# Attention and two feed-forward layers on one core: chunk 3's second-layer pass behind the first layer's passes, with seven products in both of its matmuls, and joint softmax statistics of two heads

## The chip, the core and the metric

The kernel runs on one core of one Trainium2 chip. The metric is device time in microseconds (us) of one execution. Engines are named as in the profile: PE (TensorE) multiplies matrices, PEld is its weight load, DVE (VectorE) and ACT (ScalarE) work element by element, POOL is GpSimd, SP issues the DMAs. PE accumulates in PSUM, which has eight banks of 512 float32 columns; all else lies in SBUF or DRAM.

## What is computed

The attention is causal by blocks of 64 positions, for 4 batches of 8 heads with 576 positions of 64 numbers each:

```python
scores = scale * np.matmul(q, k.transpose(0, 1, 3, 2))
mask = block_i >= block_j
scores = np.where(mask, scores, -1000000000.0)
scores = scores - np.max(scores, axis=-1, keepdims=True)
attn = np.exp(scores)
attn = attn / (np.sum(attn, axis=-1, keepdims=True) + 1e-09)
return np.matmul(attn, v)
```

Its output, 2304 tokens of 512 numbers, goes through two layers of width 2048. The first has `h = x @ w_in`, `g = h * tanh(softplus(h))`, `g @ w_out`; the second has `h = max(x @ w_in, 0)`, `h * h @ w_out`. All inputs and outputs are float32.

## The kernel before

**Numbers.** A float32 matrix is held as two float16 parts, a high and a low one, and a product takes three matmuls: high by high, low by high, high by low.

**Chunks and passes.** The tokens are cut into six chunks of 384 (`CH1`). A pass `(l, c)` takes chunk c through layer l. It has eight groups j; in each, the first matmul makes 256 of the 2048 inner columns, ACT applies the layer's function, and the second matmul adds their share to the output. `PASSES` is the order of the twelve passes, (0, 0), (0, 1), (0, 2), (1, 0), (1, 1), (0, 3), (1, 2), (1, 3), (0, 4), (0, 5), (1, 4), (1, 5), and the second matmul of a group runs one group behind the first one.

**Two ways for each matmul.** The plain way is line 1352 in the first matmul (`first_half`) and line 1464 in the second (`second_half`): 24 matmuls of 384 columns in each group. The other way replaces a 2x2 block product by seven products of blocks, with sums of blocks formed beforehand: `first_seven` (line 1385), for the passes in `SEVEN`, has 42 matmuls of 192 columns in a group; `second_seven` (line 1503), for the passes in `BOTH`, has 36 of 192 columns and 12 pieces, six of 128 and six of 64, because one of its seven products is spread over the spare columns of three accumulators. It needs seven blocks of the activation, of which DVE forms four by subtraction (line 1445) before it splits all seven, 1344 columns, into high and low part (lines 1121 to 1123 and 818); the plain way splits 768 columns. It accumulates in six banks, of which two, `bank`, otherwise serve the attention.

**Weights.** The float16 parts are kept in DRAM (`wspill`) and read for each group (`weights`, line 1246): 512 KB, or 384 KB where only three of four blocks are wanted. Block sums are formed by `upgrade` (lines 1206 to 1215), stored in `uspill` and read for each group (`sums_of`, line 1225). `UP` says in which pass which sums are formed. From pass number `KEEP` on, the sums for the second layer's first matmul stay in SBUF once read.

**Attention.** `attention_hi` (line 865) handles two heads and 384 queries in three tiles of 128. PE writes the scores of head 0 into one bank and of head 1 into the other (line 909); each head's maximum is taken by its own DVE reduction (`peak`, line 922), multiplied by the scale (`low`, line 927); ACT takes the exponential and sums it (`expo`, line 933); DVE adds a small constant (line 943), takes the reciprocal (line 945), and the result is split and transposed by DMA (`finish`, lines 953 to 958). The third tile's diagonal block is computed with the first tile, copied out of PSUM for each head (`tail`, line 791), and its maximum and sum are merged later (`merge`, line 940).

**Order.** Each step is recorded as a task with its dependencies, and a packed table, `PLAN`, holds the sequence of all tasks and the engine of each that has a choice. Each engine runs its own instructions in that order. So a step that waits holds up what is queued behind it on its engine.

## Time and profile before

| | us |
|---|---|
| median of 3 runs | 860.58 (860.36 to 862.75) |
| the profiled execution's own time | 862.35 |
| its span | 860.6 |
| PE busy | 845.9 |
| DVE busy | 757.8 |
| ACT busy | 620.8 |
| POOL busy | 62.8 |

The span runs from the first to the last instruction that was profiled; what lies around it is the difference to the execution's own time, 1.75 us. Busy time is the time in which an engine had at least one instruction in work. Matmuls overlap, so a single one's duration is longer than the time by which it delays the next one; that time is read from the starts of groups that follow each other.

### The profile page before, as it was taken

To read this page: it belongs to the slowest core of one execution; us is meant where nothing else is said; L and a number is where in the kernel's file an instruction comes from. 1 tells how busy PE (TensorE), PEld (TensorE's weight loads), DVE (VectorE), ACT (ScalarE), POOL (GpSimd) and SP (SyncE) were. 2 spreads that over 40 slices of the span, in tenths; PEclk is the share of its full clock that TensorE was granted. 3 is DMA by queue.
4 is the path that set the end of the run, shared out by engine and by line. 5 is a ranking of instruction groups with operands and counts; after the bars stand their busy time and mean duration, and the time that the engine had idled before them with its cause. 6 is when DMAs were issued, how large, how long until landed. Compare 5 with 4: busy or idle time off the path is not lost.

```text
span 860.6 us, 19000 instructions
## 1 busy us (share of the span) xinstructions
PE 845.9 (98%) x7233; PEld 606.5 (70%) x7233; DVE 757.8 (88%) x1831; ACT 620.8 (72%) x1231; POOL 62.8 (7%) x68
## 2 busy tenths in 40 slices
...
GB/s 348 385 349 196 222 242 246 288 303 309 262 280 170 284 251 205 235 287 257 277 293 335 264 230 281 231 262 195 256 242 279 180 243 190 264 229 253 190 204 79
DMA packets 163930, 217.23 MB, mean 252 GB/s; under 512 B 107520, under 2 KB 125952, under 8 KB 163840
## 3 DMA queue, kind: packets, MB, share of 16 engines
...
q14 instruction: 34, 0.28, 0.1%
...
## 4 chain that ended last, share of the span: by engine, by line
PE 76%; DVE 6%; ACT 4%; DMA 3%; issue 1%; ACTq 0%; DVEq 0%
PE acc L1464 30%; PE hp L1385 22%; PE hp L1352 11%; PE acc L1503 5%; PE bank L1018 3%; PE bank L909 3%; PE bank L1503 2%; ACT pad L933 1%; DMA qk<-in_qp_dram 1%; DMA arena<-wspill 1%; DMA wspill<-arena 1%; DVE arena L818 1%; DVE pb L818 1%; ACT L1357 1%; DMA late<-pb 1%
## 5 line engine op out<-in xcount | busy, mean ns | idle before, releaser
L1464 PE MATMUL acc<-g,arena 128*128 128x384 f16 x1560 | 300.4, 326 | 2.1 <-DVE late L1478 0.8
L1464 PEld LDWEIGHTS <-arena 128*128 128x128 f16 x1560 | 146.7, 98 | 87.2 <-issue 7.0
L1385 PEld LDWEIGHTS <-arena 128*128 128x128 f16 x1194 | 101.2, 98 | 15.3 <-DMA arena<-wspill 1.8
L1352 PE MATMUL hp<-xt,first 128*128 128x384 f16 x528 | 101.2, 326 | 0.4 <-ACT h L1357 0.3
L818 DVE SCALAR_TENSOR_TENSOR g<-h,cst,g 128x768 f16<-128x768 f32 x72 | 73.3, 1018 | 4.9 <-ACT g L1121 3.7
L1352 PEld LDWEIGHTS <-first 128*128 128x128 f16 x528 | 49.1, 97 | 40.4 <-issue 9.2
L1385 PEld LDWEIGHTS <-first 128*128 128x128 f16 x816 | 69.5, 98 | 7.2 <-issue 0.4
L1352 PE MATMUL hp<-xt,arena 128*128 128x384 f16 x384 | 73.8, 326 | 0.0
L818 DVE SCALAR_TENSOR_TENSOR pb<-pad,st,pb 128x384 f16<-128x384 f32 (+2 forms) x96 | 71.8, 751 | 1.2 <-ACT pb L953 1.1
L933 ACT ACTIVATE pad<-bank,st,sq 128x448 f32<-128x448 f32 (+1 forms) x96 | 64.9, 680 | 4.4 <-DVE st L927 3.6
L1385 PE MATMUL hp<-arena 128*128 128x192 f16 x660 | 65.8, 246 | 0.0
L1406 ACT ACTIVATE h<-h,cst 128x576 f32<-128x576 f32 x40 | 30.9, 774 | 43.0 <-DVE h L1404 39.9
L953 ACT ACTIVATE pb<-pad,st 128x640 f16<-128x640 f32 (+2 forms) x72 | 51.1, 718 | 7.5 <-DVE st L945 5.3
L1385 PE MATMUL hp<-xt,arena 128*128 128x192 f16 x534 | 54.8, 246 | 1.6 <-DMA arena<-wspill 1.6
L1357 ACT ACTIVATE h<-hp,cst 128x384 f32<-128x384 f32 x76 | 41.6, 575 | 17.2 <-PE hp L1352 14.3
L922 DVE TENSOR_REDUCE st<-bank 128x1 f32<-128x448 f32 (+1 forms) x96 | 52.5, 571 | 0.9 <-PE bank L913 0.4
L1352 PEld LDWEIGHTS <-arena 128*128 128x128 f16 x384 | 36.1, 98 | 24.2 <-issue 0.8
L1385 PE MATMUL hp<-arena,first 128*128 128x192 f16 x480 | 50.0, 246 | 0.0
L1121 ACT ACTIVATE g<-h,cst 128x768 f16<-128x768 f32 x38 | 35.4, 931 | 10.2 <-PE acc L1464 8.5
L1402 ACT ACTIVATE h<-hp,cst 128x192 f32<-128x192 f32 x40 | 16.7, 416 | 34.9 <-PE hp L1385 29.9
L1210 DVE TENSOR_TENSOR arena<-arena 128x256 f32<-128x256 f32 x96 | 41.2, 430 | 0.6
L1503 PEld LDWEIGHTS <-arena 128*128 128x128 f16 x504 | 37.5, 98 | 0.0
...
## 6 DMA issues: line engine op xcount, KB each, us to landing
...
```

The lines of the kernel that those rows point to most:

```text
L818: return sch.add("DVE", c_dve(n) + 62 * ap, lambda: nc.vector.scalar_tensor_tensor(dst(), a(), s() if ap else s, c(), op0, op1), r=r, w=w, ...
L922: t = sch.add("DVE", c_dve(o1 - o0), lambda hd=hd: nc.vector.reduce_max(st.t[:, 2 * j + hd:2 * j + hd + 1], pp.t[hd][:, o0:o1], axis=AX.X) ...
L933: t = sch.add("ACT", c_act(o1 - o0, True, 3), lambda hd=hd: nc.scalar.activation(pf[hd].t[r0:, k0:k0 + o1 - o0], view(hd)[r0:, o0:o1], AF. ...
L953: "ACT": ("ACT", c_act(n, False, 1), lambda pb=pb, pv=pv, s=s: nc.scalar.activation(pb.t[:, 0:i + 1, 0, :], pv(), AF.Copy, scale=s()), False),
L1121: "ACT": ("ACT", c_act(n, False, 1), lambda: nc.scalar.activation(dst(0), src(), AF.Copy, scale=s()), False),
L1210: plus(ENG["ts"], 256, lambda e, o=o, x=x, y=y, op=op: e.tensor_tensor(b(o), b(x), b(y), op), [], [q])
L1352: nc.tensor.matmul(out=hp.t[:, 0:n], lhsT=w.t[:, f % 2, a, 128 * k:128 * k + 128], rhs=x.t[:, c, k, 0:n], start=k == 0 and i == 0, stop=k ...
L1357: sch.add("ACT", c_act(n, True, 1), lambda f=f, o=o, hp=hp: nc.scalar.activation(h.t[:, o * n:o * n + n], hp.t[:, 0:n], (AF.Mish, AF.Relu) ...
L1385: nc.tensor.matmul(out=bank.t[:, o:o + z], lhsT=lhs, rhs=x.t[:, c, ks[k], :], start=start and k == 0 and i == 0, stop=k == 1 and i == 2, s ...
L1406: sch.add("ACT", c_act(3 * z, False, 1), lambda: nc.scalar.activation(h.t[:, z:2 * n], h.t[:, z:2 * n], fn, scale=hs()), r=[(cst, (HS, j)) ...
L1464: nc.tensor.matmul(out=acc.t[:, 0:n], lhsT=wo.t[:, f % 2, a, 128 * m:128 * m + 128], rhs=g.t[:, c, f % 2 * n:f % 2 * n + n], start=f == 0 ...
L1503: nc.tensor.matmul(out=acc[bank].t[:, o:o + c1 - c0], lhsT=lhs, rhs=g.t[:, c, z * b + c0:z * b + c1], start=j == 0 and (bank, o) in first ...
```

## The change

Chunk 3's second-layer pass (1, 3) moves from behind (1, 2) to behind (0, 5), so that the second layer's last three passes stand together, and it joins `BOTH`. `KEEP` and `UP` follow: the sums that stay are read in (1, 3), and the block sums for the second matmul are formed in the same two passes, (0, 4) and (0, 5), which are one place earlier now. The two banks become one tile of 1024 columns, and one reduction takes the maxima of both heads. One column block `st` holds the statistics of all three tiles of a pair of heads: the constant and the reciprocal of the first two tiles are taken for four columns at once, and both their splits come behind that; the third tile's two maxima are merged by one operation with the scaling; its small sum takes the constant on POOL (line 988 of the changed kernel), and DVE adds the large one. The diagonal block is copied out for both heads by one instruction. `PLAN` is a new table throughout.

```diff
@@ -46,13 +46,13 @@
-Y_AT = ["a", "p", "s", "p", "p", "s"]
-X_AT = {(0, 0): "c", (0, 1): "b", (0, 2): "c", (1, 0): "b", (1, 1): "c", (0, 3): "y", (1, 2): "z", (1, 3): "y", (0, 4): "z", (0, 5): "y", (1, 4): "z", (1, 5): "y"}
+Y_AT = ["a", "p", "s", "p", "t", "s"]
+X_AT = {(0, 0): "c", (0, 1): "b", (0, 2): "c", (1, 0): "b", (1, 1): "c", (0, 3): "y", (1, 2): "z", (0, 4): "y", (0, 5): "z", (1, 3): "y", (1, 4): "z", (1, 5): "y"}
-KEEP = 10
+KEEP = 9
 SEVEN = {(0, 3), (1, 2), (1, 3), (0, 4), (0, 5), (1, 4), (1, 5)}
-BOTH = {(1, 4), (1, 5)}
-UP = {4: [(0, 0, j) for j in range(8)], 5: [(1, 0, j) for j in range(8)], 8: [(1, 1, j) for j in range(4)], 9: [(1, 1, j) for j in range(4, 8)]}
+BOTH = {(1, 3), (1, 4), (1, 5)}
+UP = {4: [(0, 0, j) for j in range(8)], 5: [(1, 0, j) for j in range(8)], 7: [(1, 1, j) for j in range(4)], 8: [(1, 1, j) for j in range(4, 8)]}
...
@@ -675,7 +673,7 @@
-    R["xm"] = sb("xm", [128, 8], F32, 5)
+    R["xm"] = sb("xm", [128, 8], F32, 6)
...
@@ -747,7 +745,9 @@
-    bank = [psp.tile([128, 512], F32, tag=f"bank{i}", name=f"bank{i}") for i in range(2)]
+    banks = psp.tile([128, 1024], F32, tag="bank", name="bank")
+    bank = [banks[:, 512 * i:512 * i + 512] for i in range(2)]
+    pairs = banks.rearrange("p (h c) -> p h c", h=2)
...
@@ -915,76 +915,81 @@
-        both = lambda st, j, r0=0: st.t[r0:, 2 * j:2 * j + 2]
-
-        def peak(st, j, pp, o0, o1):
-            for hd in range(2):
-                t = sch.add("DVE", c_dve(o1 - o0), lambda hd=hd: nc.vector.reduce_max(st.t[:, 2 * j + hd:2 * j + hd + 1], pp.t[hd][:, o0:o1], axis=AX.X),
-                            w=[(pp, hd), (st, (j, hd))])
-                t.banks = (hd,)
-
-        def low(st, r):
-            sch.add("DVE", 69.0, lambda: nc.vector.tensor_scalar(both(st, 2), both(st, 0), sq.t[:, 5:6], None, ALU.mult),
-                    r=[(sq, 5), *r], w=[(st, 2)], lat=70.0)
-
-        def expo(st, j, pp, r0, o0, o1, pf, k0):
-            view = lambda hd: pp.t[hd] if j == 4 else pp.t[:, hd]
+        st = R["st"].new()
+        two = lambda j, n=2: st.t[:, 2 * j:2 * j + n]
+        TOP, SUM = (0, 2, 3), (4, 5, 7)
+
+        def peak(j, pp, o0, o1):
+            sch.add("DVE", 70.0 + c_dve(2 * (o1 - o0)), lambda: nc.vector.reduce_max(two(j), pairs[:, :, o0:o1], axis=AX.X),
+                    w=[(pp, 0), (pp, 1), (st, (j, 0)), (st, (j, 1))]).banks = (0, 1)
+
+        def low(j, n):
+            keys = [(st, (k, hd)) for k in range(j, j + n) for hd in range(2)]
+            sch.add("DVE", 69.0, lambda: nc.vector.tensor_scalar(two(j, 2 * n), two(j, 2 * n), sq.t[:, 5:6], None, ALU.mult),
+                    r=[(sq, 5)], w=keys, lat=70.0)
+
+        def expo(j, b, pp, o0, o1, pf, k0):
+            view = lambda hd: pp.t[:, hd] if j == 6 else pp.t[hd]
             for hd in range(2):
                 t = sch.add("ACT", c_act(o1 - o0, True, 3), lambda hd=hd: nc.scalar.activation(
-                    pf[hd].t[r0:, k0:k0 + o1 - o0], view(hd)[r0:, o0:o1], AF.Exp, bias=st.t[r0:, 4 + hd:5 + hd], scale=sq.t[r0:, 4:5],
-                    accum_out=st.t[r0:, 2 * j + hd:2 * j + hd + 1]), r=[(st, 2), (sq, 4)], w=[(pp, hd), (st, (j, hd)), (pf[hd], k0)], table="exp")
-                t.banks = (hd,) if j == 4 else ()
-
-        def merge(st, j, op, r, w):
-
-            sch.add("DVE", 69.0, lambda: nc.vector.tensor_tensor(both(st, j), both(st, j), both(st, j + 1), op), r=r, w=w)
-
-        def finish(i, st, pf):
-            sch.add("DVE", 69.0, lambda: nc.vector.tensor_scalar(both(st, 6), both(st, 4), 1e-9, 1.0 / PSC, ALU.add, ALU.mult),
-                    r=[(st, (4, 0)), (st, (4, 1))], w=[(st, 6)])
-            sch.add("DVE", 75.0, lambda: nc.vector.reciprocal(both(st, 7), both(st, 6)), r=[(st, 6)], w=[(st, 7)], lat=70.0)
+                    pf[hd].t[:, k0:k0 + o1 - o0], view(hd)[:, o0:o1], AF.Exp, bias=st.t[:, 2 * b + hd:2 * b + hd + 1], scale=sq.t[:, 4:5],
+                    accum_out=st.t[:, 2 * j + hd:2 * j + hd + 1]), r=[(st, (b, hd)), (sq, 4)], w=[(pp, hd), (st, (j, hd)), (pf[hd], k0)], table="exp")
+                t.banks = () if j == 6 else (hd,)
+
+        def finish(i, pf):
+            k = SUM[i - 2]
...
-                s = lambda hd=hd: st.t[:, 14 + hd:15 + hd]
+                s = lambda hd=hd: st.t[:, 2 * k + hd:2 * k + hd + 1]
...
-                    [(st, 7), f], [(pb, 0)])
+                    [(st, (k, hd)), f], [(pb, 0)])
-                    ALU.mult, ALU.subtract, [(st, 7), f, (pb, 0)], [(pb, 1)], 1)
+                    ALU.mult, ALU.subtract, [(st, (k, hd)), f, (pb, 0)], [(pb, 1)], 1)
...
         scale_of(R["qm"].new())
+        pfs = {}
         for i in (2, 3):
             n = tile_keys(i)
-            pp, st, pf = R["ab"].new(), R["st"].new(), [R["pf", i].new() for _ in range(2)]
+            pp, pfs[i] = R["ab"].new(), [R["pf", i].new() for _ in range(2)]
             scores(pp, (i, 0, 0, n, True), *([(4, n, 448, 576, True)] if i == 2 else []))
             if i == 2:
-                last, tail = R["st"].new(), R["tl"].new()
+                tail = R["tl"].new()
                 steps.append(halves(vs, v3, sv, R["vm"].new()))
-            peak(st, 0, pp, 0, n)
+            peak(TOP[i - 2], pp, 0, n)
             if i == 2:
-                for hd in range(2):
-                    t = copy(ENG["tail"], 128, lambda hd=hd: tail.t[:, hd], lambda pp=pp, n=n, hd=hd: pp.t[hd][:, n:n + 128], [], [(pp, hd), (tail, hd)], True)
-                    t.banks = (hd,)
-                sch.add("DVE", c_dve(256), lambda: nc.vector.reduce_max(both(last, 1), tail.t, axis=AX.X), r=[(tail, 0), (tail, 1)], w=[(last, 1)])
-            low(st, [(st, (0, 0)), (st, (0, 1))])
-            expo(st, 4, pp, 0, 0, n, pf, 0)
-            finish(i, st, pf)
+                copy(ENG["tail"], 256, lambda: tail.t, lambda n=n: pairs[:, :, n:n + 128], [], [(pp, 0), (pp, 1), (tail, 0), (tail, 1)], True).banks = (0, 1)
+                low(0, 1)
+                expo(SUM[0], 0, pp, 0, n, pfs[i], 0)
+                sch.add("DVE", c_dve(256), lambda: nc.vector.reduce_max(two(1), tail.t, axis=AX.X),
+                        r=[(tail, 0), (tail, 1)], w=[(st, (1, 0)), (st, (1, 1))])
+            else:
+                low(1, 2)
+                expo(SUM[1], 2, pp, 0, n, pfs[i], 0)
+        keys = [(st, (k, hd)) for k in (4, 5) for hd in range(2)]
+        sch.add("DVE", 70.0, lambda: nc.vector.tensor_scalar(two(4, 4), two(4, 4), 1e-9, 1.0 / PSC, ALU.add, ALU.mult), w=keys)
+        sch.add("DVE", 79.0, lambda: nc.vector.reciprocal(two(4, 4), two(4, 4)), w=keys, lat=70.0)
+        for i in (2, 3):
+            finish(i, pfs[i])
         pp, pf = R["ab"].new(), [R["pf", 4].new() for _ in range(2)]
         scores(pp, (4, 0, 0, 448, False))
-        peak(last, 0, pp, 0, 448)
-        merge(last, 0, ALU.max, [(last, 1), (last, (0, 0)), (last, (0, 1))], [(last, 0)])
-        low(last, [(last, 0)])
-        expo(last, 5, tail, 0, 0, 128, pf, 448)
-        expo(last, 4, pp, 0, 0, 448, pf, 0)
-        merge(last, 4, ALU.add, [(last, (5, 0)), (last, (5, 1))], [(last, (4, 0)), (last, (4, 1))])
-        finish(4, last, pf)
+        peak(3, pp, 0, 448)
+        keys = [[(st, (k, hd)) for hd in range(2)] for k in (1, 3, 6, 7)]
+        sch.add("DVE", 69.0, lambda: nc.vector.scalar_tensor_tensor(two(3), two(3), sq.t[:, 5:6], two(1), ALU.mult, ALU.min),
+                r=[(sq, 5), *keys[0]], w=keys[1], lat=70.0)
+        expo(6, 3, tail, 0, 128, pf, 448)
+        sch.add("POOL", 492.0, lambda: nc.gpsimd.tensor_scalar(two(6), two(6), 1e-9, 1.0 / PSC, ALU.add, ALU.mult), w=keys[2])
+        expo(7, 3, pp, 0, 448, pf, 0)
+        sch.add("DVE", 69.0, lambda: nc.vector.scalar_tensor_tensor(two(7), two(7), 1.0 / PSC, two(6), ALU.mult, ALU.add), r=keys[2], w=keys[3])
+        sch.add("DVE", 75.0, lambda: nc.vector.reciprocal(two(7), two(7)), w=keys[3], lat=70.0)
+        finish(4, pf)
...
@@ -1809,10 +1814,10 @@
-PASSES=[(0, 0), (0, 1), (0, 2), (1, 0), (1, 1), (0, 3), (1, 2), (1, 3), (0, 4), (0, 5), (1, 4), (1, 5)]
+PASSES=[(0, 0), (0, 1), (0, 2), (1, 0), (1, 1), (0, 3), (1, 2), (0, 4), (0, 5), (1, 3), (1, 4), (1, 5)]
...
@@ -1820,7 +1825,7 @@
-ATT = [[2, 1, 0, 0.0, 0.093], [3, 2, 1, 1.938, 4.83], [4, 5, 7, 0.035, 1.615], [5, 6, 8, 0.044, 1.181]]
+ATT = [[2, 1, 0, 0.0, 0.093], [3, 2, 1, 1.938, 4.83], [4, 4, 7, 0.035, 1.615], [5, 5, 8, 0.044, 1.181]]

```

Line numbers of the changed kernel are five higher than before from `second` on. Three places show what the new table does to the order.

DVE inside the pass (1, 3). Before, `g` is the activation of the group, split whole; `h` is that of the next one:

```order
L1397 TENSOR_TENSOR h_7240<-first,hp_123 128x192
L1398 TENSOR_TENSOR h_7240<-h_7240,hp_123 128x192
L1286 TENSOR_TENSOR xs<-xs 128x2x192 x3
L1404 TENSOR_TENSOR h_7240<-first,hp_123 128x384
L1286 TENSOR_TENSOR xs<-xs 128x2x192
L1123 TENSOR_SCALAR g_7302<-h_7240,cst_6196 128x768
L818 SCALAR_TENSOR_TENSOR g_7302<-h_7240,cst_6196,g_7302 128x768
```

Now, with the activation in `pad` and its split in `pt`:

```order
L1403 TENSOR_TENSOR pad<-pad,hp_123 128x192
L1450 TENSOR_TENSOR pad<-pad 128x192
L1121 TENSOR_SCALAR cst_7136<-cst_7136 128x1
L1450 TENSOR_TENSOR pad<-pad 128x192
L1344 TENSOR_SCALAR cst_7136<-wst_1503,cst_7136 128x16
L830 TENSOR_REDUCE xm_8201<-xs 128x1
L1409 TENSOR_TENSOR pad<-first,hp_123 128x384
L818 SCALAR_TENSOR_TENSOR pt<-pad,cst_7136,pt 128x1344
L1450 TENSOR_TENSOR pad<-pad 128x192 x2
```

The split has 1344 columns in place of 768, and subtractions of 192 columns (L1450) stand between.

POOL while the attention of a middle chunk runs. Before, only splits of activations (`g`) and of queries and keys (`q`) and a square stand there:

```order
L1122 TENSOR_SCALAR arena<-late,cst_6196 128x384
L1122 TENSOR_SCALAR g_6346<-h_6259,cst_4183 128x768
L1122 TENSOR_SCALAR g_6495<-h_6382,cst_4183 128x768
L895 TENSOR_SCALAR q_15_6545<-qk,sq_6503 128x384
L1368 TENSOR_TENSOR h_7042<-h_7042 128x768
```

Now the small sums of the third tile (`st`) stand between them:

```order
L1127 TENSOR_SCALAR g_3688<-h_3645,cst_2304 128x768
L988 TENSOR_SCALAR st_3695<-st_3695 128x2
L1127 TENSOR_SCALAR g_4095<-h_4067,cst_2971 128x768
L988 TENSOR_SCALAR st_3970<-st_3970 128x2
L1127 TENSOR_SCALAR g_4335<-h_4298,cst_2971 128x768
L988 TENSOR_SCALAR st_4341<-st_4341 128x2
```

There are 16 such small sums, one for each pair of heads and chunk of the long kind, and each waits its turn behind the split ahead of it.

DVE at the very end of the program, where the last pass's accumulators are read out. Before, the two attention banks are read behind the three small pieces:

```order
L1527 SCALAR_TENSOR_TENSOR qk<-acc_12_10234,cst_9592,pt 128x2x192
L1543 SCALAR_TENSOR_TENSOR pt<-acc_13_10225,cst_9592,pt 128x128
L1543 SCALAR_TENSOR_TENSOR pt<-acc_13_10227,cst_9592,pt 128x128
L1543 SCALAR_TENSOR_TENSOR pt<-acc_12_10234,cst_9592,pt 128x128
L1527 SCALAR_TENSOR_TENSOR qk<-bank_126,cst_9592,pad 128x2x192
L1527 SCALAR_TENSOR_TENSOR pt<-acc_12_10234,cst_9592,pt 128x384
L1527 SCALAR_TENSOR_TENSOR qk<-bank_125,cst_9592,pt 128x2x192
```

Now:

```order
L1532 SCALAR_TENSOR_TENSOR vs<-acc_12_10274,cst_9668,pt 128x2x192
L1548 SCALAR_TENSOR_TENSOR pt<-acc_13_10265,cst_9668,pt 128x128
L1532 SCALAR_TENSOR_TENSOR vs<-bank,cst_9668,pad 128x2x192
L1548 SCALAR_TENSOR_TENSOR pt<-acc_13_10267,cst_9668,pt 128x128
L1548 SCALAR_TENSOR_TENSOR pt<-acc_12_10274,cst_9668,pt 128x128
L1532 SCALAR_TENSOR_TENSOR pt<-acc_12_10274,cst_9668,pt 128x384
L1532 SCALAR_TENSOR_TENSOR vs<-bank,cst_9668,pt 128x2x192
```

The first of the two banks is read ahead of two of the small pieces, and both are one tile now.

## Rows read from the trace of the kernel before

**Rows 1.** The page's first part: busy us (share of the span) and instructions.

```profile
PE 845.9 (98%) x7233; PEld 606.5 (70%) x7233; DVE 757.8 (88%) x1831; ACT 620.8 (72%) x1231; POOL 62.8 (7%) x68
```

**Rows 2.** Busy us of each engine in stretches of the span; columns in the first row.

```profile
core 0: us, PE busy (x) PEld busy (x) DVE busy (x) ACT busy (x) POOL busy (x), PEclk, DMA share, GB/s
0.00:50.00 50.00, 44.95 (x265) 33.43 (x266) 41.12 (x145) 41.45 (x142) 5.72 (x14) 1.00 0.97 363
50.00:152.00 102.00, 100.98 (x613) 58.16 (x612) 98.21 (x260) 100.11 (x205) 5.39 (x5) 1.00 0.85 243
152.00:300.00 148.00, 147.52 (x1059) 86.61 (x1058) 143.23 (x335) 136.51 (x249) 23.71 (x23) 1.00 0.94 272
300.00:400.00 100.00, 99.22 (x720) 58.27 (x719) 90.93 (x216) 71.92 (x151) 3.48 (x4) 1.00 0.93 246
400.00:500.00 100.00, 99.38 (x922) 72.51 (x920) 98.37 (x236) 91.26 (x167) 3.33 (x3) 1.00 1.00 286
500.00:588.00 88.00, 86.43 (x841) 64.46 (x840) 77.12 (x202) 67.15 (x146) 4.45 (x5) 1.00 1.00 247
588.00:700.00 112.00, 112.00 (x1020) 89.11 (x1019) 83.60 (x172) 46.27 (x76) 7.78 (x7) 1.00 0.69 241
700.00:861.00 161.00, 155.41 (x1810) 144.00 (x1808) 125.23 (x272) 66.09 (x101) 8.95 (x7) 0.99 0.57 201
```

**Rows 3.** Timeline of PE in late passes: start, duration, line, operation, count.

```profile
670.66 1.63 PE L1464 MATMUL acc<-g,arena 128*128 128x384 f16 x9
672.12 0.66 PE L1385 MATMUL hp<-xt,arena 128*128 128x192 f16 x6
...
793.23 1.65 PE L1385 MATMUL hp<-arena,first 128*128 128x192 f16 x18
794.71 0.66 PE L1503 MATMUL bank<-pt,arena 128*128 128x192 f16 x6
...
787.27 1.17 PE L1503 MATMUL acc<-pt,arena 128*128 128x128 f16 x18
788.27 0.66 PE L1385 MATMUL hp<-xt,first 128*128 128x192 f16 x6
```

**Rows 4.** DVE by line and shape: count, busy us, mean ns of one, idle before.

```profile
L922 DVE TENSOR_REDUCE st<-bank 128x1 f32<-128x448 f32 x64 | 37.7, 615 | 0.3 <-PE bank L909 0.3
L922 DVE TENSOR_REDUCE st<-bank 128x1 f32<-128x320 f32 x32 | 14.8, 482 | 0.6 <-PE bank L913 0.4 <-PE bank L837 0.2
L927 DVE TENSOR_SCALAR st<-st,sq 128x2 f32<-128x2 f32 x48 | 11.1, 230 | 0.6
L943 DVE TENSOR_SCALAR st<-st 128x2 f32<-128x2 f32 x48 | 8.8, 187 | 1.0 <-ACT pad L933 0.7
L945 DVE RECIPROCAL st<-st 128x2 f32<-128x2 f32 x48 | 7.5, 158 | 0.2
L940 DVE TENSOR_TENSOR st<-st 128x2 f32<-128x2 f32 x32 | 4.9, 154 | 0.8 <-ACT pad L933 0.6
```

**Rows 5.** The same view: DVE's work for the second matmul, seven products and plain.

```profile
L1445 DVE TENSOR_TENSOR pad<-pad 128x192 f32<-128x192 f32 x64 | 21.9, 354 | 1.9 <-ACT pad L1367 1.1
L818 DVE SCALAR_TENSOR_TENSOR pt<-pad,cst,pt 128x1344 f16<-128x1344 f32 x16 | 25.8, 1615 | 1.0 <-ACT pt L1121 0.4 <-POOL pt L1122 0.3
L818 DVE SCALAR_TENSOR_TENSOR g<-h,cst,g 128x768 f16<-128x768 f32 x72 | 73.3, 1018 | 4.9 <-ACT g L1121 3.7 <-POOL g L1122 0.5
```

**Rows 6.** Timeline of PE: the first product of pass (1, 2), with the idle time before.

```profile
513.10 0.67 PE L1385 MATMUL hp<-xt,arena 128*128 128x192 f16 x6 [1.57 <-DMA arena<-wspill]
```

**Rows 7.** Timeline of the end: PE's last group and DVE's last operations.

```profile
853.76 1.65 PE L1503 MATMUL bank<-pt,arena 128*128 128x192 f16 x18
...
855.08 0.87 DVE L1543 SCALAR_TENSOR_TENSOR pt<-acc,cst,pt 128x128 f32<-128x128 f32 x3
855.86 0.61 DVE L1527 SCALAR_TENSOR_TENSOR qk<-bank,cst,pad 128x384 f32<-128x384 f32 x1
...
857.10 0.62 DVE L1527 SCALAR_TENSOR_TENSOR qk<-bank,cst,pt 128x384 f32<-128x384 f32 x1
```

**Rows 8.** POOL by line and shape: a memset of one column, a split of 768 columns.

```profile
L1122 POOL TENSOR_SCALAR g<-h,cst 128x768 f16<-128x768 f32 x13 | 12.7, 980 | 167.7 <-ACT h L1406 70.1 <-DVE h L1398 50.0 <-ACT h L1367 23.0
...
L1880 POOL MEMSET const-float32-1.0<- 128x1 f32 x1 | 0.1, 98 | 0.0
```

**Rows 9.** Weight loads of line 1503: duration min, median, max in ns.

```profile
L1503 PEld LDWEIGHTS <-arena x504: 97/98/98, 752.8 to 855.1; 128*128 128x128 f16 x168
```

More of the change, by code (lines that the diff above doesn't have):

```diff
@@ new lines @@
+    "d0%(wgYpm_7kNj1(VsczEx8~6Y|(pVvhLB><zcy72FY61?9e;qc3G(tb*ui3|CZ@y9Vhq55`9V6>yvW5JRx_;BXS*UR_dA3Mds)g(n1EH`An{Kli#(e^hNXe"
+    "db13ZU-c=x_oqHBm&^OCoujSgR=o9?T*%5Ma+3^}_VTw5A_lKXSDDJ%bEUVmL&jYFUMtEB{YWavQ*xSogI&LB3;chZe1Z2SXk+;aKTILVj+algKh`vocl1M@"
+    "#NDH13^w$UbL0y7SbNFSa-P(aPxVv1NM1v?TcoO7fUKAGeJv{^^m=(-`=Y^Ut;I=iY8UePDIJAppCHyx%9X6lm8N9Y3wVBn{z`tlpxx2?AtLw&5o|5r=^NTv"
+    "I+L?cpwr#*lD<rga?K;;-zjo2F)7kgrWh|@AWv&Q&fHFHN}<_#QlyXS-R!=LNS-CV@b-gxyIw{H_18wG5Sg3gK6ajr);*+1*2)4RSg3C2HDuo|^5hD=n(Vnk"
```

181 lines of the change are left out of this document (87 added, 94 removed).

## The prediction

> **What bounds the kernel now.** I read the page's first part first: PE is busy for 845.9 of 860.6 us, DVE for 757.8, ACT for 620.8 [rows 1]. So PE sets the pace, and time can be won in two ways only: less work on PE's path, or less waiting by PE. How the waiting is spread is told by the busy time in stretches of the span [rows 2]. The reader is to subtract PE's column from the length of each stretch: 5.05 us idle in the first 50 us (filling), then 1.02, 0.48, 0.78, 0.62 and 1.57 up to 588, nothing at all in 588 to 700, and 5.59 in the last stretch, which holds the drain. Interior waits from 50 to 588 are therefore 4.47 us together; that is the whole stock which a better order could save. The granted clock stands at 0.99 or 1.00 in every stretch, the 2.4 GHz level, so no term below needs a clock. DVE's column says where it could decide: 98.21 of 102, 143.23 of 148 and 98.37 of 100 us while the attention runs, but 83.6 of 112 behind it and 125.23 of 161 in the last two passes. The timeline of PE gives the price of each way of multiplying by the starts of groups that follow each other [rows 3], and DVE's work by line and shape gives the prices of the statistics [rows 4] and of the second matmul's blocks [rows 5].
>
> **Seven products in (1, 3): the large term.** Nine matmuls of 384 columns take 672.12 − 670.66 = 1.46 us, 0.162 each. Eighteen of 192 take 794.71 − 793.23 = 1.48, 0.082 each. Eighteen of the narrow class, six of which are full 192 columns and twelve pieces of 128 and 64, take 788.27 − 787.27 = 1.00; less six at 0.082, the twelve pieces cost 0.51 [rows 3]. A plain group of the second matmul is 24 × 0.162 = 3.89 us, one with seven products 36 × 0.082 + 0.51 = 3.47. Eight groups give 8 × 0.42 = **3.4 us less on PE**. PE is the bound in that place, so this comes off the end one for one, unless PE waits instead.
>
> **What (1, 3) asks of DVE.** Four subtractions in eight groups are 32 × 0.34 = 10.9 us, and the split grows from 1018 to 1615 ns, 8 × 0.6 = 4.8 [rows 5]: 16 us, with ACT's half of the split beside it. I cost it at nothing. The cover is DVE's spare time where the pass goes: two passes of exactly this kind already run from 700 on, with DVE at 125.23 of 161 us and PE gapless until the drain [rows 2], and the pass that leaves the attention's end takes its DVE work along. Without that cover up to 16 us would stand against it.
>
> **Loads and SP's queue.** The move carries the loads of its groups with it. Eight loads of the second matmul's plain parts shrink from 512 to 384 KB, eight loads of its block sums come in, and the first matmul's sums, which now stay from the ninth place on, are read once as before but serve three passes standing together. So bytes rise by 8 × (512 − 128) KB = 3.1 MB at most, less the eight reads of first-matmul sums that (1, 3) had made for itself. The DMA share is 0.69 and 0.57 in the two late stretches against 1.00 in 400 to 588 [rows 2]: (1, 3) leaves the full stretch and goes into the free one. I take 0. The block sums for the second matmul are now formed one place earlier, against the attention's end, where DVE has 88 − 77.12 = 11 us free [rows 2].
>
> **Joint statistics of two heads.** Removed from DVE: 96 maxima (37.7 + 14.8 us), 48 scalings (11.1), 48 constants (8.8), 48 reciprocals (7.5) and 32 merges (4.9), 84.8 us [rows 4]. Added: a maximum over two times the columns is in no row; from 320 to 448 columns a single one grows by (615 − 482)/128 = 1.04 ns a column, so 448 more cost 0.466 and the joint one 1.08 us; two times 320 cost 0.482 + 0.333 = 0.815 [rows 4]. The other bound is two full ones, 1.23 and 0.96. With 32 and 16 of them that is 47.6 us (54.8 at the other bound); with 32 scalings at 0.23, 16 four-wide constants at 0.19, 32 reciprocals at 0.16, and 32 operations of the scaling's kind for the merges, another 22.9. So DVE is relieved by 84.8 − 70.5 = 14 us, or 7 at the other bound; I take 14, since the slope is measured. Beside it ACT issues 16 copies of the diagonal block in place of 32. None of this is on PE's path. It reaches the end only through the interior waits, of which the row that I show waits for a transfer, not for DVE [rows 6]. Bounds: 0 and 4.47 us of gain. I take **0.5**, near the lower end. What speaks against more: one tile for both banks lets the maximum start only when both heads' scores are there, and holds both until it is over.
>
> **The third tile's small sum on POOL.** Sixteen operations of two columns; POOL shows one of one column at 98 ns and splits of 768 at 980 [rows 8]. Between these bounds I take 0.1 to 0.5 each and cost it at nothing: the small exponential that feeds it stands ahead of the large one on ACT, whose time hides the rest. Behind it, if it is late, stand DVE's large sum, the reciprocal and all that is queued on DVE.
>
> **The end.** PE's last product is over at 853.76 + 1.65 = 855.41 and DVE's last read at 857.72 [rows 7]: 2.31 us. The first bank is now read ahead of two of the small pieces, and as one tile with the other it may have to wait for the bank's last product. Behind 855.41 would then stand 0.61, two pieces of 0.29, 0.62 and the middle one of some 0.6, together 2.4, with what passes between them up to 2.7. I take **0.3 more**; the bounds are 0 and 0.4.
>
> **Sum.** −3.4 − 0.5 + 0.3 = −3.6 us. The profiled execution took 862.35, so it would take 858.75. That execution lies 1.77 above the median of the runs, 860.58; from the median the forecast is **857.0**, with its own range 855.5 to 858.3 (all of the statistics' doubt up to 1.5 below, the end and small new waits of 1.3 above). A measurement of this kernel tells 0.3% from no change, 2.6 us: faster is below 858.0, slower above 863.2.
>
> **Rivals.** *New waits give it back* (0.26). (1, 3) had stood ahead of the pass (0, 4) with eight groups of 42 × 0.082 + 3.89 = 7.3 us [rows 3], 59 us in which weights could be read ahead and splits and sums formed. Now (0, 4) and its block sums come at once, in the stretch where the DMA share is 1.00 and PE already waits 1.57 us for `arena` [rows 2, 6]. Two more such waits cost 3.1: 860.58 − 3.4 + 3.1 = 860.3, no change. Against it: 11 us of DVE are free there and behind 588 nothing waits.
>
> *All interior waits go* (0.07). If 14 us on DVE clear the stretches in which it is full, the 4.47 go with the 3.4: 860.58 − 7.9 + 0.3 = 853.0. Against it: the largest of them is a DMA's.
>
> *POOL holds up DVE* (0.08), the case that ends slower. POOL runs in order; a small sum that arrives behind a split of 768 columns waits up to 0.98 us [rows 8], and DVE, in order too, waits with it while it is 97% full. Sixteen such places give back the whole 3.4 from 0.21 us each. At a mean of 0.5, half a split, 8 us: 860.58 − 3.6 + 8 = 865. For it: the order shows these sums standing right between such splits. Against it: POOL is busy for 62.8 of 860.6 us [rows 1], so few of them meet a split at work.
>
> *Weight loads set the pace* (0.02). A load of line 1503 takes 98 ns [rows 9], longer than the 0.082 of its matmul. A group with seven products has 48 loads where a plain one has 24; were loads the limit, it would take 48 × 0.098 = 4.70 us against 3.89, so 8 × 0.81 = 6.5 us more, 867. Against it stands the row of eighteen loads with their products in 1.00 us, 56 ns each [rows 3]: loads overlap each other. The Trainium skill, "Perfetto Trace Analysis", section "Identifying the Most-Contended Engine", holds the busy time of matmuls a bad measure, since they are pipelined, and asks for the busy share of weight loads instead; by that rule the second matmul's new form, which doubles the loads, would be the dearer one. The trace disagrees here: PEld rises from 89.11 of 112 to 144 of 161 us in the late passes, and PE still runs without a gap [rows 2].
>
> *The change doesn't do what it says* inside the rest (0.57 with the forecast): were (1, 3)'s second matmul still plain, line 1464 would keep its 8 × 24 = 192 matmuls, and the time would stay near 860.
>
> **How the numbers follow.** Forecast 0.57 (of which 0.50 below 858.0), new waits 0.26 (0.04 below, 0.21 within), all waits gone 0.07, POOL and loads 0.10. Faster 0.61, same 0.28, slower 0.11, the last hundredth from new waits beyond 863.2. The range is 854.0 to 860.8: it takes in the forecast and the usual end of the first rival; some 0.07 lies outside below and 0.12 above.
>
> **What would show it.** In the changed profile, line 1508 (1503 before) must have half as many matmuls again (three passes for two), and the PE groups the same spacings as now; PE idle 588 to the drain must stay near 0. The joint maxima should take about 1.08 and 0.82 us; if nearer 1.23, DVE's relief halves. PE's idle in 400 to 600 tells the first rival, DVE's waits for POOL's small sums the third, and the stretch from PE's last product to the end should be 0.1 to 0.4 longer. I am wrong if PE waits more than 2 us longer in the interior, or if a group of the second matmul in (1, 3) takes more than 3.5 us.

## The result and the profile after

The changed kernel takes 868.68 us (median of 4 runs, 867.50 to 870.79) against 861.41 for the kernel before: a ratio of 1.0087, interval 1.0072 to 1.0102. The forecast was 857.0, so it missed by 11.7 us and on the wrong side. The profiled execution took 867.5, its span is 865.4.

The page's first part after the change:

```profile
PE 845.8 (98%) x7425; PEld 617.2 (71%) x7425; DVE 768.6 (89%) x1751; ACT 623.7 (72%) x1227; POOL 61.3 (7%) x79
```

PE is busy as long as before [rows 1], though 3.4 us of matmuls are gone. Where it lost time is told by the same stretches as before, columns as in [rows 2]:

```profile
0.00:50.00 50.00, 42.26 (x247) 31.38 (x248) 37.87 (x130) 37.21 (x130) 4.05 (x13) 1.00 0.91 335
50.00:152.00 102.00, 98.13 (x566) 56.82 (x566) 94.08 (x238) 96.36 (x196) 6.62 (x10) 1.00 0.75 229
152.00:300.00 148.00, 146.48 (x1053) 86.52 (x1052) 139.06 (x300) 133.19 (x247) 19.64 (x24) 1.00 0.97 275
300.00:400.00 100.00, 99.71 (x734) 58.13 (x733) 94.32 (x195) 75.09 (x157) 6.26 (x7) 1.00 0.92 247
400.00:500.00 100.00, 99.59 (x887) 71.03 (x886) 96.75 (x214) 86.49 (x157) 2.95 (x6) 1.00 0.99 281
500.00:588.00 88.00, 87.43 (x874) 65.73 (x872) 79.84 (x189) 70.57 (x153) 6.99 (x8) 1.00 1.07 263
588.00:700.00 112.00, 112.00 (x1007) 88.33 (x1005) 88.45 (x189) 46.41 (x75) 6.73 (x6) 1.00 0.69 243
700.00:866.00 166.00, 160.19 (x2073) 159.25 (x2070) 138.21 (x301) 78.41 (x119) 8.08 (x6) 0.99 0.59 194
```

The late stretches are as forecast: no idle PE from 588 to 700, and 5.81 us in the last stretch, 0.6 of it beyond the span's end. The loss is at the other end. In the first 50 us PE is idle for 7.74 us instead of 5.05, from 50 to 152 for 3.87 instead of 1.02, and DVE and ACT do less there as well. So no engine was overloaded there; they waited for each other. What PE waited for in the first 152 us, by line and releaser (total us, times, longest), kernel before:

```profile
PE acc L1054 <- DMA qk<-in_qk_dram: 4.1, 1, 4.1
PE bank L1054 <- ACT xs L791: 0.4, 1, 0.4
PE hp L1352 <- ACT h L1357: 0.3, 1, 0.3
...
```

and after the change:

```profile
PE acc L1059 <- DMA qk<-in_qk_dram: 4.1, 1, 4.1
PE bank L1097 <- ACT pt L791: 1.2, 2, 0.6
PE bank L884 <- ACT pad L934: 0.9, 1, 0.9
PE bank L1059 <- DVE wst L1176: 0.6, 1, 0.6
PE acc L1082 <- DVE pt L825: 0.5, 1, 0.5
PE bank L1170 <- DVE st L1064: 0.5, 1, 0.5
PE bank L909 <- ACT xs L791: 0.5, 1, 0.5
PE bank L1059 <- DVE xs L793: 0.5, 1, 0.5
...
```

The first load is the same. The new waits are almost all at `bank`, on lines that the change did not touch: the short attention of chunk 1 (L1059, L1097), the weights' norms (L1170), the scale sums (L884) and the scores of the long attention (L909). One such wait in full, the maxima of one pair of heads in the short attention; first DVE, then PE, both after the change:

```profile
19.63 0.55 DVE L1064 TENSOR_REDUCE st<-bank 128x2 f32<-128x384 f32 x1
...
21.93 0.22 DVE L1065 TENSOR_REDUCE st<-bank 128x1 f32<-128x64 f32 x1 [0.77 <-PE bank L1060]
```

```profile
18.19 0.98 PE L1059 MATMUL bank<-vs 128*128 128x192 f32 x6
19.01 0.22 PE L1060 MATMUL bank<-small,above 128*128 128x128 bf16 x1
...
20.86 0.98 PE L1059 MATMUL bank<-vs 128*128 128x192 f32 x6
21.68 0.22 PE L1060 MATMUL bank<-small,above 128*128 128x128 bf16 x1
```

Chunk 1's pairs of heads use the two banks in turn. Both reductions belong to one pair, whose scores were complete at 19.23. The second one still waited until 21.90, when PE had finished the next pair's scores in the other half. DVE was through with its work in between at 21.16 and stood idle for 0.77 us. The same pair in the same order on two tiles is shown with experiment e7 below: there the reduction runs while PE writes the next pair's scores.

To follow the lag through the program, each matmul is given the median distance to the next start that its line and shape has in the trace of before; these are added up in each kernel's own sequence, and the times are compared at which a kernel and the one before have the same sum of PE work done. Positive is later than before, in us (estimates from the starts of matmuls, good to about 1 us, at 480 less so); the last column is the start of the last matmul, which holds the 3.4 us that seven products save. The experiments, described in the next section, stand in the same table.

| kernel | 40 us | 80 | 140 | 280 | 480 | 600 | last |
|---|---|---|---|---|---|---|---|
| after | 4.9 | 6.8 | 8.9 | 9.2 | 9.3 | 8.2 | 4.8 |
| e1_one_tile | 3.4 | 4.3 | 6.2 | 8.6 | 9.6 | 9.7 | 9.8 |
| e2_old_start | 3.8 | 5.1 | 8.1 | 7.5 | 8.8 | 7.7 | 4.7 |
| e3_new_start | 1.0 | 0.9 | 0.7 | 1.1 | 2.3 | 2.7 | 2.9 |
| e4_move_only | -0.2 | 0.6 | 2.5 | 2.1 | 3.1 | 3.3 | 0.0 |
| e6_move_old_order | -0.1 | -0.6 | -0.6 | 1.0 | 0.1 | 1.2 | -2.2 |
| e7_split_start | 0.9 | 0.5 | 2.1 | 1.7 | 1.5 | 1.6 | -1.8 |
| e8_split_old_start | 0.1 | -0.3 | 2.8 | 3.9 | 5.2 | 4.8 | 1.8 |
| e9_split_old_order | 0.0 | -0.5 | 2.9 | 5.9 | 10.7 | 13.6 | 10.2 |
| e10_two_tiles | 1.0 | 0.5 | 0.9 | 0.0 | -1.0 | -2.0 | -5.0 |
| e11_before_split | -0.2 | -0.4 | 0.4 | 2.8 | 3.8 | 6.9 | 6.9 |
| e12_sum_on_dve | 4.9 | 6.8 | 9.6 | 9.7 | 10.6 | 9.1 | 5.7 |

Each row is one execution, the profiled one. In e3 and e4 it took 3.2 and 3.1 us more than the kernel's median, in e8 and e11 1.7, in e9 1.3 and in e6 1.1; in the changed kernel it took 1.2 less and in e1 1.0 less, elsewhere it lies within 0.6; in the kernel before, the reference, it took 0.9 more than 861.41. A difference between two rows counts only as far as the medians bear it out.

So the change is 4.9 us late by 40 us of work, where nothing but the tile and the order differs (the first joint maximum starts at 89.3 us of the span), and some 9 late from 140 to 480; then the last passes give 3.4 back.

### The profile page after: what moved, and what is told of

It reads as the page before. It is cut to its first block, busy times and chain, and to the rows that moved or that the text cites. A ratio compares the mean times of both kernels' runs of the same rounds, so it can differ in the third digit from the quotient of the medians.

```text
span 865.4 us, 19310 instructions
## 1 busy us (share of the span) xinstructions
PE 845.8 (98%) x7425; PEld 617.2 (71%) x7425; DVE 768.6 (89%) x1751; ACT 623.7 (72%) x1227; POOL 61.3 (7%) x79
## 4 chain that ended last, share of the span: by engine, by line
PE 65%; ACT 7%; DVE 7%; DMA 3%; issue 2%; ACTq 0%; DVEq 0%
PE acc L1469 21%; PE hp L1390 19%; PE hp L1357 10%; PE acc L1508 7%; PE bank L1508 3%; PE bank L1023 3%; PE bank L909 2%; ACT pad L934 2%; DMA wspill<-arena 1%; DMA arena<-in_w_dram 1%; DVE arena L1211 1%; DVE arena L1215 1%; DMA out_dram<-late 1%; ACT g L1126 1%; DVE st L923 1%
## 5 line engine op out<-in xcount | busy, mean ns | idle before, releaser
L1469 PE MATMUL acc<-g,arena 128*128 128x384 f16 x1464 | 281.7, 326 | 0.0
L1469 PEld LDWEIGHTS <-arena 128*128 128x128 f16 x1464 | 138.0, 98 | 80.2 <-issue 4.9
L1390 PEld LDWEIGHTS <-arena 128*128 128x128 f16 x1008 | 85.3, 98 | 12.9 <-issue 1.7
L1390 PEld LDWEIGHTS <-first 128*128 128x128 f16 x1008 | 85.3, 98 | 7.0 <-issue 1.2
L1357 PEld LDWEIGHTS <-first 128*128 128x128 f16 x528 | 49.2, 98 | 41.5 <-issue 10.6
L1390 PE MATMUL hp<-arena,first 128*128 128x192 f16 x672 | 70.3, 246 | 0.4 <-DVE h L1403 0.4
L818 DVE SCALAR_TENSOR_TENSOR g<-h,cst,g 128x768 f16<-128x768 f32 x64 | 64.8, 1012 | 3.2 <-ACT g L1126 2.9
L948 ACT ACTIVATE pb<-pad,st 128x384 f16<-128x384 f32 (+2 forms) x81 | 57.1, 719 | 4.7 <-DVE cst L1308 1.9
L1357 PEld LDWEIGHTS <-arena 128*128 128x128 f16 x384 | 36.2, 98 | 25.3 <-issue 2.1
L1390 PE MATMUL hp<-arena 128*128 128x192 f16 x492 | 52.1, 246 | 0.0
L1508 PEld LDWEIGHTS <-arena 128*128 128x128 f16 x696 | 51.9, 98 | 0.0
L923 DVE TENSOR_REDUCE st<-bank 128x2 f32<-128x896 f32 (+1 forms) x48 | 47.8, 996 | 1.9 <-ACT h L1362 0.5
L1508 PE MATMUL acc<-pt,arena 128*128 128x192 f16 (+2 forms) x522 | 45.0, 232 | 0.0
L818 DVE SCALAR_TENSOR_TENSOR pt<-pad,cst,pt 128x1344 f16<-128x1344 f32 x24 | 38.8, 1615 | 4.3 <-ACT pt L1126 2.5
```

The costliest lines, as they stand in the source:

```text
L818: return sch.add("DVE", c_dve(n) + 62 * ap, lambda: nc.vector.scalar_tensor_tensor(dst(), a(), s() if ap else s, c(), op0, op1), r=r, w=w, ...
L923: sch.add("DVE", 70.0 + c_dve(2 * (o1 - o0)), lambda: nc.vector.reduce_max(two(j), pairs[:, :, o0:o1], axis=AX.X), w=[(pp, 0), (pp, 1), (s ...
L948: "ACT": ("ACT", c_act(n, False, 1), lambda pb=pb, pv=pv, s=s: nc.scalar.activation(pb.t[:, 0:i + 1, 0, :], pv(), AF.Copy, scale=s()), False),
L1357: nc.tensor.matmul(out=hp.t[:, 0:n], lhsT=w.t[:, f % 2, a, 128 * k:128 * k + 128], rhs=x.t[:, c, k, 0:n], start=k == 0 and i == 0, stop=k ...
L1390: nc.tensor.matmul(out=bank.t[:, o:o + z], lhsT=lhs, rhs=x.t[:, c, ks[k], :], start=start and k == 0 and i == 0, stop=k == 1 and i == 2, s ...
L1469: nc.tensor.matmul(out=acc.t[:, 0:n], lhsT=wo.t[:, f % 2, a, 128 * m:128 * m + 128], rhs=g.t[:, c, f % 2 * n:f % 2 * n + n], start=f == 0 ...
```

## The experiments

Theory **tile**: as one tile, the banks are guarded as one, so an engine that uses one half waits for engines at the other half. Rival **order**: the new table has a worse sequence at the start.

**One tile alone**, in the kernel before:

```diff
-    bank = [psp.tile([128, 512], F32, tag=f"bank{i}", name=f"bank{i}") for i in range(2)]
+    banks = psp.tile([128, 1024], F32, tag="bank", name="bank")
+    bank = [banks[:, 512 * i:512 * i + 512] for i in range(2)]
```

> The kernel before with one edit: the two attention banks are allocated as one tile of 1024 columns; operations, order and passes stay. After the change PE is 4.9 us late by 40 us of its work and 8.2 late by 140, and 3.4 come back in the last passes. Theory tile: accesses of one engine to one half now wait for other engines' accesses to the other half, and the short attention of chunk 1, which alternates between the banks, is serialised in the first 100 us. It expects 5 to 8 us more than before, about 867, nearly all of it by 150 us. Theory order: the new table sets a worse sequence for the start, and the tile is innocent. It expects the time of before, 861.4, within 1 us.

Measured: 873.08 us against 861.46, ratio 1.0139 (1.0115 to 1.0163). The same operations in the same order lose 12 us. That is more than theory tile had said, and not nearly all of it by 150 us: the lag goes on growing in the long attention, from 6.2 to 9.8. Its first two stretches look like the changed kernel's:

```profile
0.00:50.00 50.00, 42.82 (x252) 31.50 (x253) 38.12 (x134) 39.31 (x131) 5.72 (x14) 1.00 0.93 349
50.00:152.00 102.00, 98.19 (x571) 56.12 (x569) 95.17 (x255) 97.50 (x202) 5.36 (x5) 1.00 0.79 238
```

**The order of the start, both ways**:

```diff
 e2: kernel after
-PLAN: the new table from its first step
+PLAN: the first 425 steps of the table before, then the rest in the new table's order
 e3: kernel before
-PLAN: the old table from its first step
+PLAN: the first 433 steps of the new table, then the rest in the old table's order
```

> The changed kernel with the first 425 steps in the order of the kernel before (some 57 us of PE's work; these steps are the same in both kernels); one tile for the banks stays. Theory order: the lag of 5.5 us by then goes, about 863. Theory tile: the lag stays, 868 within 1.5.

> The kernel before with the first 433 steps in the changed kernel's order; the two banks stay two tiles. Theory order: about 5 us more than before, 866 to 867. Theory tile: the time of before, 861.4, within 1.5 us.

Measured: e2 866.82, ratio 1.0062 (1.0039 to 1.0085), and e3 863.16, ratio 1.0015 (1.0002 to 1.0028). The old start under one tile is still 5.1 us late by 80 us; the new start on two tiles costs 0.9. By the medians the order of the start has a share of some 2 us (868.68 to 866.82, and 861.46 to 863.16, 0.3 above what theory tile allowed for e3); the tile has the rest.

**The moved pass alone**, first in the changed kernel's order (behind the first 425 steps), then in the order of before up to 468 us of work:

```diff
-PASSES=[... (1, 2), (1, 3), (0, 4), (0, 5), (1, 4), (1, 5)]
+PASSES=[... (1, 2), (0, 4), (0, 5), (1, 3), (1, 4), (1, 5)]
-BOTH = {(1, 4), (1, 5)}
+BOTH = {(1, 3), (1, 4), (1, 5)}
```

with `KEEP`, `UP`, `X_AT`, `Y_AT`, `ATT` and `xm` as in the change.

> Of the change only the moved pass (1, 3) with seven products, KEEP and UP; attention statistics for each head and two tiles for the banks as before; start in the order of before, the rest in the changed kernel's order. Both theories expect the 3.4 us of the prediction's first term and no lag at the start: 857 to 859 against 861.4. If the pass in its new place costs new waits, it would stand at 860 or above.

> The moved pass with seven products alone, two tiles, statistics for each head, and now the order of the kernel before up to the start of pass (1, 2) (some 468 us of PE's work), the changed kernel's from there. The run with the move alone was 3.3 us late at 600 us of PE's work, with the order that was made for other statistics. If that order caused it, the lag goes and the prediction's first term stands alone: 861.5 - 3.4 = 858, at most 858.5. If the move itself costs waits (loads, block sums one place earlier), they remain: 859 to 860.

Measured: e4 859.24, ratio 0.9974 (0.9963 to 0.9984); e6 859.60, ratio 0.9978 (0.9966 to 0.9991). Both are faster than before, by 2 us and not by 3.4. In the table each gains some 3.4 between 600 and the end, and each had lost some before; e4's row, of an execution 3.1 us above its median, makes that loss too large. In e6 the lag is 0.1 at 480 and 1.2 at 600, behind the place where its two orders are joined. PE's two longest waits there, between 470 and 530 us, are 1.5 us (L838) and 0.7 (L910), both at `bank` on steps of the attention and none on a load; before, the longest one there was 1.6 us for `arena` [rows 6]. That speaks for the joint rather than for the moved pass's loads, but whether the move makes a part of the missing 1.1 us was not separated. The times of e4 and e6 don't differ, so the expectation that the order explains e4's lag is not borne out by the times.

**Two tiles at the start, one behind it**, in the changed kernel. The tiles are exchanged in front of the first scores of the long attention, where no step is using them:

```diff
-    banks = psp.tile([128, 1024], F32, tag="bank", name="bank")
+    bank = [early.enter_context(tc.tile_pool(name=f"early{i}", bufs=1, space=bass.MemoryType.PSUM)).tile([128, 512], F32, tag=f"bank{i}", name=f"bank{i}") for i in range(2)]
...
+            if t.banks == (0, 1) and pairs is None:
+                early.close()
+                banks = ctx.enter_context(tc.tile_pool(name="joint", bufs=1, space=bass.MemoryType.PSUM)).tile([128, 1024], F32, tag="bank", name="bank")
...
```

> The changed kernel, its order untouched; the banks are two tiles until the last step of chunk 1's short attention, and one tile from the first scores of the long attention on. Theory tile: nearly the whole lag of 7.8 us by 140 us goes, 861 to 862.5. Rival, the joint statistics (maxima that wait for both heads, small sums on POOL behind splits): the start changes nothing, 866 or above.

> As the run before, and the first 425 steps in the order of the kernel before. From the run that gave the kernel before the new start (0.7 to 1 us late), theory tile expects about 1 us less than the run before: 860 to 861.5. If the order of the start matters only under one tile, the same time as the run before.

> All parts of the change (moved pass, joint statistics), two tiles at the start and one after it, the order of the kernel before up to pass (1, 2). Theory tile: 3.4 us from the pass, 0 to 0.5 from the relief of DVE, 0 to 1 lost to the one tile in the long attention: 857.5 to 859. Rival, joint statistics cost time of their own in the long attention: 860 or above, with a lag that grows between 150 and 550 us.

Measured: e7 861.35, ratio 0.9995 (0.9985 to 1.0005): 7.3 us less than the changed kernel's 868.68, as theory tile said, by an edit that touches neither the order nor the joint statistics; the rival, joint statistics, had 866 or above. PE's stretches are near those of before again:

```profile
0.00:50.00 50.00, 45.43 (x262) 33.85 (x263) 41.48 (x142) 41.51 (x145) 5.11 (x13) 1.00 0.97 361
50.00:152.00 102.00, 100.29 (x607) 57.81 (x606) 96.07 (x237) 98.28 (x195) 7.32 (x10) 1.00 0.77 235
```

And the second reduction of the pair that was shown above, first DVE, then PE, waits no more; it runs at 20.98, while PE writes the next pair's scores into the other bank:

```profile
20.44 0.63 DVE L794 COPY pt<-hp 128x448 f32<-128x448 f32 x1
20.98 0.22 DVE L1066 TENSOR_REDUCE st<-bank 128x1 f32<-128x64 f32 x1
```

```profile
20.72 0.98 PE L1060 MATMUL bank<-vs 128*128 128x192 f32 x6
21.54 0.22 PE L1061 MATMUL bank<-small,above 128*128 128x128 bf16 x1
```

The other two went against the expectation. e8 with the old start takes 862.42, ratio 1.0009 (0.9996 to 1.0022): level at 80 us, its row loses 5 by 480, but its median is only 1.1 us above that of e7. e9 with the old order as far as pass (1, 2) takes 871.34, ratio 1.0115 (1.0102 to 1.0128): level at 80 us, it is 13.6 late by 600. That is the sign that the rival named for e9, joint statistics with a cost of their own. But e7 has the same statistics, and its lag does not grow from 140 to 600 (2.1 and 1.6). So it is the old order that does not suit them under one tile; how much of the 13.6 us is the tile was not separated, since no run has this order and these statistics on two tiles.

**One tile in the long attention**, from both sides. e10 is the changed kernel on two tiles throughout; a joint maximum and a joint copy become two instructions at the same place:

```diff
-    banks = psp.tile([128, 1024], F32, tag="bank", name="bank")
-    bank = [banks[:, 512 * i:512 * i + 512] for i in range(2)]
-    pairs = banks.rearrange("p (h c) -> p h c", h=2)
+    bank = [psp.tile([128, 512], F32, tag=f"bank{i}", name=f"bank{i}") for i in range(2)]
...
-            sch.add("DVE", 70.0 + c_dve(2 * (o1 - o0)), lambda: nc.vector.reduce_max(two(j), pairs[:, :, o0:o1], axis=AX.X),
+            sch.add("DVE", 70.0 + c_dve(2 * (o1 - o0)), lambda: [nc.vector.reduce_max(st.t[:, 2 * j + hd:2 * j + hd + 1], pp.t[hd][:, o0:o1], axis=AX.X) for hd in range(2)],
...
```

e11 is the kernel before with the exchange of tiles as in e7; one small step of the weights' norms stands earlier, ahead of the exchange.

> The changed kernel and its order, with two tiles for the banks throughout; the joint maxima and the joint copy are two instructions each again, one for each head, at the place of the joint one, and all other joint statistics stay. DVE has about 7 us more to do than with joint maxima (1.08 to 1.23 us for 32, 0.82 to 0.96 for 16). Theory tile: the lag of the start goes, and what is left of it between 150 and 550 us too, since no half waits for the other any more: 858 to 861. If the joint maxima are worth more than the one tile costs in the long attention, it is slower than the run with the split start, 862 or above.

> The kernel before, with two tiles at the start and one tile from the first scores of the long attention on (one small step of the weights' norms moved ahead of the switch). Statistics for each head. The run with one tile from the start lost 6.2 us by 140 us of PE's work and 3.5 more by 500. Theory tile expects the second part alone: 3 to 4 us more than before, a lag that begins after 140 us. If the start alone matters, the time of before.

Measured: e10 857.46 against 861.93, ratio 0.9947 (0.9926 to 0.9968), the fastest of all and faster than both kernels. e11 867.50, ratio 1.0067 (1.0048 to 1.0085). e10 is a little below what theory tile had said, e11 above it (3 to 4 us more). So one tile costs in the long attention too: e7 and e10 differ by 3.9 us at the median and 3.2 in the table's last column, though DVE is busy for 769.7 us in e10 and 767.2 in e7. How much of this is the guard and how much a joint maximum's wait for both heads, e10 does not tell, since it takes both away. e11, which has no joint maximum, shows that the guard alone costs there: 5.6 us at the median, 6.9 in the table. The three stretches of e10 up to the end of the attention:

```profile
0.00:50.00 50.00, 45.18 (x262) 33.73 (x263) 41.33 (x143) 41.42 (x145) 5.09 (x13) 1.00 0.97 361
50.00:152.00 102.00, 101.39 (x614) 58.05 (x613) 97.69 (x250) 99.21 (x202) 7.28 (x10) 1.00 0.78 236
152.00:588.00 436.00, 434.66 (x3564) 283.61 (x3563) 413.93 (x944) 363.26 (x717) 38.24 (x46) 1.00 0.98 266
```

Its PE is idle for 1.34 us from 152 to 588. Before it was 3.45, the four stretches of [rows 2] together.

**The small sum on POOL**, in the changed kernel:

```diff
-        sch.add("POOL", 492.0, lambda: nc.gpsimd.tensor_scalar(two(6), two(6), 1e-9, 1.0 / PSC, ALU.add, ALU.mult), w=keys[2])
+        sch.add("POOL", 492.0, lambda: nc.vector.tensor_scalar(two(6), two(6), 1e-9, 1.0 / PSC, ALU.add, ALU.mult), w=keys[2])
```

> The changed kernel with the third tile's small sum on DVE in place of POOL, at the same place of the order. The prediction's rival on POOL expects several us less, towards 861. Theory tile expects no difference beyond 1 us, 867.5 to 869.5: in the changed kernel's trace no DVE instruction waits for that sum.

Measured: 868.81, ratio 1.0079 (1.0057 to 1.0102), the changed kernel's time. DVE now does the sums itself (191 ns each), and nothing is won: POOL did not cause the loss.

## Why the prediction was wrong

The step that failed is the sentence on the maximum in the statistics' term: "one tile for both banks lets the maximum start only when both heads' scores are there, and holds both until it is over". It saw the tile, for the one operation that the change rewrote, and gave it no price; the bounds, "0 and 4.47 us of gain", left out a loss. What had to be asked is who else uses the two banks. The short attention of chunk 1 puts one pair of heads into each in turn, so that PE can fill one while DVE and ACT read the other; norms and scale sums use spare columns of one of them. As one tile all of these wait for each other. By the medians this cost 7.3 us at the start (868.68 in the changed kernel, 861.35 in e7) and 3.9 in the long attention (861.35 to 857.46), 11.2 together; the table's last column has 6.6 and 3.2. The sign of being wrong that the prediction named came true, PE idle for 6.66 us from 50 to 588 instead of 4.47, but the growth lies in 50 to 152 and not in 400 to 600, where its first rival looked. No rival had this cause. The two that ended slower, POOL's sums (865) and weight loads (867), named times not far from the measured one by other mechanisms, which the runs did not show.

The guard itself is not idle caution. The Trainium skill, "PSUM — Partial Sum Buffer", section "PSUM bank collisions raise a hardware error", asks for PSUM to be guarded by bank and quadrant of partitions, not by address, because two engines at once in one bank and quadrant raise an error and spoil data even at different columns. That rule needs no wait between two banks; the waits seen here (0.77 us in the example above, gone in e7) come from a tile that covers both. What happens without a guard no run here shows.

The other steps, one by one:

**Seven products, 3.4 us: right.** From 600 us of work to the last matmul the lag falls from 8.2 to 4.8, and by 3.0 to 3.4 us in every other kernel with the moved pass. The groups keep their spacing; PE's last ones after the change:

```profile
856.05 1.17 PE L1508 MATMUL acc<-pt,vs 128*128 128x192 f16 x18
857.05 1.65 PE L1508 MATMUL acc<-pt,arena 128*128 128x192 f16 x18
858.54 0.66 PE L1508 MATMUL bank<-pt,late 128*128 128x192 f16 x6
...
859.53 0.66 PE L1508 MATMUL bank<-pt,arena 128*128 128x192 f16 x6
```

18 with the pieces in 1.00 us, 18 of 192 columns in 1.49, as in [rows 3].

**DVE's cover and the loads: right, with some 1 us open.** DVE does 138.21 us in the last 166 and PE has no gap ahead of the drain; from 300 to 588 PE is idle for 1.27 us instead of 2.97. The rival of new waits for weights fell: PE's idle time from 400 to 588 fell from 2.19 to 0.98 us. Only the 1.1 us that e4 and e6 lack stay open. **Weight loads as the limit: rightly held unlikely.** PEld is busy for 159.25 of the last 166 us with PE's spacing unchanged, so the loads set no slower pace. The Trainium skill ("Perfetto Trace Analysis", "Identifying the Most-Contended Engine") asks to judge by the busy share of weight loads together with the share of peak FLOP/s; here the first of the two is 79% from 588 to 700 us (88.33 of 112) and 96% in the last stretch, with PE gapless in both up to the drain.

**Statistics: durations right, worth too low.** DVE's maxima and small sums after the change:

```profile
L923 DVE TENSOR_REDUCE st<-bank 128x2 f32<-128x896 f32 x32 | 34.7, 1084 | 0.9 <-PE bank L909 0.3 <-PE bank L913 0.2
L923 DVE TENSOR_REDUCE st<-bank 128x2 f32<-128x640 f32 x16 | 13.1, 819 | 1.0 <-ACT h L1362 0.5 <-PE bank L1273 0.4
L928 DVE TENSOR_SCALAR st<-st,sq 128x2 f32<-128x2 f32 x16 | 3.7, 230 | 0.1
L977 DVE TENSOR_SCALAR st<-st 128x4 f32<-128x4 f32 x16 | 3.1, 191 | 2.1 <-ACT pad L934 2.1
L990 DVE SCALAR_TENSOR_TENSOR st<-st 128x2 f32<-128x2 f32 x16 | 2.7, 171 | 0.7 <-ACT pad L934 0.7
```

1084 and 819 ns stand against 1.08 and 0.815 us worked out from the slope. The operations listed in [rows 4] were busy for 84.8 us; those in their place are busy for 69.6 after the change, a relief of 15 us where 14 was taken, and for 73.4 in e10. But DVE's relief was the smaller matter. On two tiles, with some 11 of the 15 us, e10 gains 4.5 us at the median and 5.0 in the table, 1.1 to 1.6 beyond the pass's 3.4 where I took 0.5; how much of it is the order and how much the statistics was not separated. The rival that all interior waits go did not come about: e10, the nearest to it, still has 1.95 us of idle PE from 50 to 588.

**POOL's sum: right.** It takes 333 ns on average, between the bounds of 0.1 and 0.5 taken (single ones 191 to 789); DVE's large sum (L990, above) waits for ACT alone:

```profile
L988 POOL TENSOR_SCALAR st<-st 128x2 f32<-128x2 f32 x16 | 5.3, 333 | 231.3 <-ACT pad L934 184.8 <-DVE arena L798 46.4
```

**The end: right in bounds, too high in value.** PE's last product is over at 859.53 + 0.66 = 860.19, DVE's last read at 862.54, 2.35 us later against 2.31 before [rows 7]; I took 0.3 more.

```profile
859.83 0.35 DVE L1548 SCALAR_TENSOR_TENSOR pt<-acc,cst,pt 128x128 f32<-128x128 f32 x1
860.22 0.62 DVE L1532 SCALAR_TENSOR_TENSOR vs<-bank,cst,pad 128x384 f32<-128x384 f32 x1
860.76 0.60 DVE L1548 SCALAR_TENSOR_TENSOR pt<-acc,cst,pt 128x128 f32<-128x128 f32 x2
...
861.92 0.62 DVE L1532 SCALAR_TENSOR_TENSOR vs<-bank,cst,pt 128x384 f32<-128x384 f32 x1
```

The first bank's read starts when DVE is through with the read in front of it (859.83 + 0.35 = 860.18), and no wait is shown ahead of it: the last product is over at 860.19, so the joined tile had next to nothing to delay here.

Without the one tile the change is faster, as forecast: e10 takes 857.46. That this lies so near to 857.0 is in part luck. The kernel before stood at 861.93 beside e10 and at 860.58 in the forecast, so e10 gains 4.5 us where 3.6 was forecast, and its maxima are taken for each head.
